# The last four chunks of tile 3 in seven products, in a linear-attention and SwiGLU kernel

## The chip, the cores and the metric

The kernel runs on one core of one Trainium2 chip. The metric is the device time of one execution in microseconds. Before the change the median of three runs is 218.54 us (217.64 to 218.71).

## The reference

Two stages follow each other. The first is linear attention with decay: 4 batches, 8 heads, 768 positions, head dimension 64. In blocks, each head computes a masked and decayed product of q and k, applies it to v, adds q times a running state, and updates the state with k and v:

```python
intra = np.einsum('bhic,bhjc->bhij', qb, kb) * Dmask[None]
intra = np.einsum('bhij,bhjd->bhid', intra, vb)
inter = np.einsum('bhid,bhde->bhie', qb * lam_pow[None], kv_state)
out[:, :, sl] = intra + inter
kv_state = lam_block[None, :, None, None] * kv_state + np.einsum('bhsd,bhse->bhde', kb_dec, vb)
```

Its output, as 3072 tokens of 512 features, is the input of the second stage, a gated feed-forward block of inner width 1536:

```python
g = x @ w_gate
silu = g * (1.0 / (1.0 + np.exp(-g)))
val = x @ w_val
return (silu * val @ w_out).astype(np.float32)
```

## The kernel before

**Groups and tiles.** The attention is done in twelve groups (0 to 11) of 256 tokens, the feed-forward block in six tiles (0 to 5) of 512 tokens. Tile t needs the attention of groups 2t and 2t+1; its input is `xt`. PE works through one list written out by hand: while tile t is in the feed-forward block, the attention of the groups of tile t+1 is put between its steps.

**Attention of a group g.** `load_group` issues the loads of k, q and v (lines 115 and 122), on SP's queue except k of group 11, which ACT issues (`KACT`, line 325). `cast_scaled` (line 277) makes bf16 copies, k on ACT (line 281) and q, scaled, on VectorE or, for groups listed in `QP` (line 275, empty), on GpSimd (line 283); then SP issues a transposing DMA (line 271) that writes `qkt`. `v_scale` (line 258) scales v, mostly on GpSimd. On PE, `scores` (line 376 for groups from 6 on) multiplies q and k, and the masks (line 381) go to VectorE, put off in the list `later`; `inter` (line 502) multiplies q with the state, `intra` (line 515) the masked scores with v; `upd_mm` (line 408) computes the update of the state. ACT copies the update (line 430), GpSimd adds it to the state (line 463), and casts of the state go to `kvn` (lines 443 and 445), for groups 8, 9 and 10 on ACT, queued in `kvq` and let out by `kv_flush` (line 447). `core_a` is `kv_flush`, `inter` and a small guard copy; `core_b` is the waiting masks, `intra` and `evac` (line 527), which writes `xt`. `attend(g)` (line 863) is `core_a(g)`, then `upd_mm`, `upd_copy` and `scores` of g+1, then `core_b(g)` and `state(g+1)`.

**Feed-forward, plain steps.** The inner width has twelve chunks of 128 (`FC`), six in each half (`FH`). A step of a tile does one chunk, `ffn_fc` (line 580): four matmuls of 512 columns for the gate (line 558), Silu on ACT (line 562), four matmuls for the value (line 574), and on VectorE the multiply that writes `h` (line 577). PSUM has eight banks, taken in turn.

**Feed-forward, seven products.** `ffn_unit(t, j, ...)` (line 686) does four chunks at once, 2j and 2j+1 of each half, as a product of two 2x2 block matrices in seven block products in place of eight. Each product is eight matmuls of 256 columns (line 703), four for the gate and four for the value. It needs sums of blocks of the weights (`w_combo`, line 651, n = 0 to 3, on VectorE), sums of blocks of `xt` (`x_combo`, line 672, n = 0 to 3, VectorE), and copies and adds between products: the A products copied bank to bank (line 737) and the E products to `es` (line 740) on ACT, adds on VectorE (lines 745 and 753), four Silus (line 730) on ACT, three multiplies on VectorE and one on GpSimd (line 733). The weight sum n = 3 overwrites a block of the weights, so the plain chunks that use this block must be done before it. `early` and `mid` are functions called after the E products and ahead of the last product. Tiles 4 and 5 are done in three such units each; tiles 0 to 3 in plain steps.

**Output.** For tiles 1 to 5 `out_units` (line 775) multiplies `h` with the output weights, also in seven products per group (line 793), with sums of blocks of `h` (`h_combo`, line 625, line 640) that wait in the list `trickle` and are let out by `drip`.

**What orders the work around the change.** Steps get a number in the order in which they are made; `at(n, fn, ...)` puts a call after step n. Lines 1114 to 1138 make the twelve steps of tiles 2 and 3; tile 3 takes its chunks in an order that goes through both halves two by two (line 1115). `WS` (line 1099) names the step after which each weight sum is computed (301 is step 1 of tile 3, 112 the thirteenth step from the second half of tile 1 on), `AT` (line 1113) the steps after which `attend` is called: for tile 3, `attend(8)` after step 5 and `attend(9)` after step 10. After the loop `out_units(2)` follows (line 1184), with sums for tile 4 let out between its products, and then the units of tile 4 (from line 1201).

Of the kernel before, what the change touches and what calls it, by code (L numbers as in the profile page):

```python
# [9 lines left out]
BF16 = mybir.dt.bfloat16  # L10
# [27 lines left out]
def _body(ctx, tc, nc, q, k, v, lam, moe_w_gate, moe_w_val, moe_w_out, out):  # L38
    B, H, S, D = q.shape
    HP = H // 2  # L40
    BLK = 128
# [4 lines left out]
    FC = DFF // 128  # L46
    FH = FC // 2
# [30 lines left out]
    ring = [0]  # L78

    primed = {}  # L80
# [26 lines left out]
    st = {}  # L107
# [164 lines left out]
                          in_=t.rearrange("p a s x -> p (a s x)"), transpose=True)  # L272
        st[("qkt", g)] = tt

    QP = ()

    def cast_scaled(g, eng=nc.vector):
        eng = nc.gpsimd if g in QP else eng
# [388 lines left out]

    xs = {}
    SY = 1
    XS0 = 4  # L670

    def x_combo(t, n, g):


        xt = st[("xt", t)]
        g = slice(0, 2) if g is None else slice(g, g + 1)
        b11, b12 = xt[:, g, 0:KH, 0], xt[:, g, 0:KH, 1]
        b21, b22 = xt[:, g, KH:MC, 0], xt[:, g, KH:MC, 1]
        if t not in xs:
            pool, tag = (qkt_pool, "qkt") if t == XS0 else (raw_pool, "raw")  # L680
            xs[t] = pool.tile([128, 3, 2, KH, BLK], BF16, name="xs", tag=tag)
        x = [xs[t][:, m, g] for m in range(3)]
        o, i0, i1 = ((x[0], b12, b11), (x[1], b22, x[0]), (x[2], b21, x[1]), (b12, b22, b12))[n]
        nc.vector.tensor_tensor(out=o, in0=i0, in1=i1, op=ALU.subtract)

    def ffn_unit(t, j, bk, early=None, mid=None, dr=(0, 0, 2)):
# [7 lines left out]
        A, E, Bb = [[banks[k] for k in bk[2 * m:2 * m + 2]] for m in range(3)]  # L694
# [5 lines left out]
        def product(i, o, lhs, rhs, start=False):  # L700
            for fi in range(2):
                for c in range(KH):
                    nc.tensor.matmul(o[:, fi * 256:fi * 256 + 256], lhs(i, c, 2 * j + fi), rhs(c),  # L703
                                     start=(start and fi == 0 and c == 0), stop=(c == KH - 1),
                                     skip_group_check=True)
# [10 lines left out]
        def xb(k, r):  # L716
            return lambda c: xt[:, :, KH * k + c, r]
# [18 lines left out]
            product(i, A[i], wa(0, 0), xb(0, 0), True)  # L736
            nc.scalar.copy(out=Bb[i], in_=A[i])
        for i in range(2):
            product(i, E[i], wa(0, 1), xb(0, 1), True)
            nc.scalar.copy(out=es[i], in_=E[i])  # L740
        if early:
            early()
# [264 lines left out]
    def at(n, fn, *a):  # L1007
        plan.setdefault(n, []).append((fn, a))
# [86 lines left out]
    at(s2, h_combo, 1, 0, 1)  # L1095
    at(s2, wo_combo, 3)

    outs = []
    WS = [(x, n, i, 0, 3) for x, n, i in ((110, 0, 0), (112, 0, 1), (206, 1, 0), (210, 1, 1), (301, 2, 0), (303, 2, 1))] + [(308, 3, 0, 0, 2), (309, 3, 1, 0, 2)]
    XC = 8  # L1100
    D0 = (0, 0, 3)
    D1 = (0, 0, 3)
    D5 = 0
    D2 = (0, 0, 2)
    M2 = (1, 1, 0, 2, 1, 2, 2)
# [1 line left out]
    KAGE = 3  # L1107
    KM = 2
    A8 = 5
    A9 = 10  # L1110
    C11 = None
    sns = {0: s1a, 1: s1b + s2h}
    AT = {2: (7, 10), 3: (A8, A9)}
    for t in range(2, 4):
        order = [c for j in range(FC // 4) for c in (2 * j, 2 * j + 1, FH + 2 * j, FH + 2 * j + 1)]
        sn = [step(t, fc, 2 if t == 2 and fc < NH else 0) for fc in (range(FC) if t == 2 else order)]
        sns[t] = sn
        if t == 2:
            at(sn[4], ahead, 6)
        for j, g in ((4 if t == 2 else 0, 2 * t + 3), (8 if t == 2 else 6, 2 * t + 4)):  # L1120
            at(sn[j], cast_scaled, g)
            at(sn[j], load_group, g + 1)
            if g > 7:
                at(sn[1 + j], v_scale, g, nc.gpsimd, 0, H // 2)
                at(sn[(1 if t == 2 else 2) + j], v_scale, g, nc.gpsimd, H // 2, H)
        for i in range(2):
            at(sn[AT[t][i]], attend, 2 * t + 2 + i)
        if t == 2:
            at(sn[4], out_units, 1, (0,), False, 2)
            at(sn[5], out_rest, 1, (0,), 2, 4)  # L1130
            at(sn[6], out_rest, 1, (0,), 4, 7)
            at(sn[5], v_scale, 7, nc.vector)
            at(sn[8], out_units, 1, (1,), False, 2)
            at(sn[9], out_rest, 1, (1,), 2, 7)
            at(sn[9], h_combo, t, (0, 2))
        else:
            at(sn[7], h_combo, t, (0, 2))
        at(sn[11], h_combo, t, 2)
    sn = sns[3]
    if C11 is not None:  # L1140
        at(sn[C11], cast_scaled, 11)
    XM = (1, 1)
    W3L = ()
    TR2 = "cxwh"
    for x, n, i, j0, j1 in WS:
        at(sns[x // 100][x % 100], w_combo, i, n, (j0, j1))
    if not XM[0]:
        for n in (0, 3, 1, 2):
            at(sn[XC], x_combo, 4, n, 0)

    for n, (t, fc, b0, b1) in enumerate(steps):
        if t >= 1 and t + 1 < NG // 2 and ("xt", t + 1) not in st:
            new_xt(t + 1)
        ffn_fc(t, fc, b0, b1)
        kvq_now.append(0)
        kv_flush(KAGE, KM)
        run_later(pace.get(n, 2 if len(later) > 1 else 1))
        todo = plan.get(n, [])
        busy = [f for f, x in todo if f in (attend, ahead, cast_scaled, v_scale)]
        if not busy:  # L1160
            drip(2 if len(trickle) > 4 else 1)
# [12 lines left out]

    def x_soon(t, g):
# [3 lines left out]
              c=[soon(cast_scaled, 11)] if C11 is None else [],  # L1179
# [38 lines left out]
    t = NG // 2 - 1  # L1218
# [38 lines left out]
```

## Time and profile before

| What | Value |
| --- | --- |
| Median of three runs | 218.54 us (217.64 to 218.71) |
| Profiled execution, time | 218.1 us |
| Its span | 216.3 us |
| Granted TensorE clock, mean | 1.0 |
| HBM read and written | 28.31 MB and 6.29 MB |
| Tile 3's twelve steps on PE, with `attend(8)` and `attend(9)` | 111.9 to 135.6 us |
| `out_units(2)` on PE | 135.6 to 144.7 us |
| Tile 4's first two units on PE | 144.7 to 160.2 us |

How to read the profile: times are in microseconds from the start of the span. PE is TensorE's matmuls, PEld its weight loads, DVE VectorE, ACT ScalarE, POOL GpSimd, SP the engine that issues most DMAs; a name with q after it is the engine's sequencer, which issues its DMAs. In the slices each digit is the busy share of one fortieth of the span, in tenths. A row of a timeline has the start, the duration, the engine, the line of the kernel, the operation, what it writes and reads with the shape, the number of merged instructions, and in brackets how long the engine sat idle before it and what ended that. Matmuls overlap in these rows, so start to start is what a stream of them takes.

### The profile page before, as it was taken

How to read it: one execution, taken by the hardware profiler on the slowest of the kernel's cores; microseconds unless marked ns; L12 is line 12 of the kernel's file. 1: busy time of each engine (PE TensorE's matmuls, PEld its weight loads, DVE VectorE, ACT ScalarE, POOL GpSimd, SP SyncE). 2: the span in 40 equal slices, each digit the busy share in tenths (PEclk: the TensorE clock that was granted, in tenths of full speed). 3: DMA queues.
4: the chain of work that ended last, by engine and by line, in shares of the span. 5: the costliest groups of instructions: out<-in, count | busy, mean ns of one | idle time of the engine just before them, and what ended most of it. 6: DMA issues, size and time to landing. Idle time of an engine off the chain costs nothing.

```text
span 216.3 us, 6883 instructions
## 1 busy us (share of the span) xinstructions
PE 209.8 (97%) x2813; PEld 153.3 (71%) x2816; DVE 149.5 (69%) x267; ACT 129.1 (60%) x280; POOL 92.3 (43%) x126
## 2 busy tenths in 40 slices
PE   8899999999999999999999999999999999999994
PEld 4666455888887447666754545888888888888883
DVE  1774447576677989775478988886797379961760
ACT  5788577666545254638368478754872766636522
POOL 6684755818498240685962336510740022200200
PEclk9999999999999999999999999999999999999999
DMA  6999999999999878999678899481000500005014
GB/s 189 346 354 345 378 337 321 290 249 232 315 352 151 191 214 190 257 186 238 168 169 236 203 230 215 103 225 68 2 5 3 194 0 3 0 3 194 0 52 146
DMA packets 88320, 39.76 MB, mean 184 GB/s; under 512 B 57698, under 2 KB 83938, under 8 KB 88290
## 3 DMA queue, kind: packets, MB, share of 16 engines
q1 hardware_dynamic: 84978, 38.22, 64.9%
q10 hardware_dynamic: 3312, 1.11, 2.0%
q8 instruction: 22, 0.36, 0.7%
q14 instruction: 8, 0.07, 0.1%
HBM read 28.31 MB, written 6.29 MB: 160 GB/s over the span
## 4 chain that ended last, share of the span: by engine, by line
PE 73%; DVE 7%; DMA 6%; SPq 5%; ACT 3%; issue 2%; POOL 2%; POOLq 1%; DVEq 0%
PE bank L793 20%; PE bank L703 15%; PE bank L558 13%; PE bank L574 13%; DMA woraw<-in_moe_w_out_dram 4%; PE bank L593 4%; SPq L122 2%; DMA qraw<-in_q_dram 2%; SPq L247 2%; DVE ws L666 2%; DVE h L577 1%; PE bank L515 1%; PE bank L146 1%; DVE wt L623 1%; PE bank L502 1%
## 5 line engine op out<-in xcount | busy, mean ns | idle before, releaser
L577 DVE TENSOR_TENSOR h<-sil,bank 128x256 bf16<-128x256 bf16 (+1 forms) x67 | 34.8, 531 | 26.3 <-PE bank L574 18.0
L558 PE MATMUL bank<-xt,wg_sb 128*128 128x256 bf16 (+1 forms) x268 | 52.5, 319 | 0.0
L574 PE MATMUL bank<-xt,wv_sb 128*128 128x256 bf16 (+1 forms) x268 | 52.4, 319 | 0.0
L562 ACT ACTIVATE sil<-bank 128x256 bf16<-128x256 f32 (+1 forms) x67 | 31.7, 479 | 23.7 <-PE bank L558 16.8
L574 PEld LDWEIGHTS <-wv_sb 128*128 128x128 bf16 x268 | 26.0, 98 | 15.8 <-DVE wv_sb L988 0.5
L558 PEld LDWEIGHTS <-wg_sb 128*128 128x128 bf16 x268 | 25.2, 98 | 13.8 <-DVE xt L527 0.2
L258 POOL TENSOR_TENSOR v_s<-v,dec 128x512 bf16<-128x512 f32 (+1 forms) x18 | 24.1, 1356 | 24.0 <-DMA v<-in_v_dram 16.0
L733 POOL TENSOR_TENSOR h<-sil,es 128x512 bf16<-128x512 bf16 x6 | 7.0, 1163 | 50.0 <-ACT sil L730 50.0
L793 PEld LDWEIGHTS <-h 128*128 128x128 bf16 x240 | 23.3, 98 | 3.4 <-issue 0.3
L793 PE MATMUL bank<-wo_sb,h 128*128 128x256 bf16 x180 | 21.6, 273 | 0.1
L793 PEld LDWEIGHTS <-hs 128*128 128x128 bf16 x180 | 17.6, 98 | 2.9
L357 DVE TENSOR_TENSOR ssb<-bank,causal 128x512 bf16<-128x512 f32 x24 | 15.4, 681 | 1.8 <-PE bank L350 1.8
L745 DVE TENSOR_TENSOR bank<-bank,es 128x512 f32<-128x512 f32 x12 | 7.8, 693 | 11.4 <-PE bank L703 10.1
L703 PEld LDWEIGHTS <-ws 128*128 128x128 bf16 x144 | 13.8, 97 | 2.3 <-issue 0.2
L793 PE MATMUL bank<-wt,hs 128*128 128x256 bf16 x120 | 15.0, 272 | 0.0
L730 ACT ACTIVATE sil<-bank 128x512 bf16<-128x512 f32 x18 | 10.7, 596 | 7.0 <-POOL h L733 4.6
L463 POOL TENSOR_TENSOR kvf<-kvs,ups 128x256 f32<-128x256 f32 x8 | 6.5, 813 | 19.1 <-ACT ups L430 19.1
L733 DVE TENSOR_TENSOR h<-sil,bank 128x512 bf16<-128x512 bf16 x18 | 12.2, 682 | 1.4 <-ACT sil L730 1.4
L703 PE MATMUL bank<-xs,ws 128*128 128x256 bf16 x96 | 12.8, 272 | 0.0
L527 ACT CAST xt<-bank 128x512 bf16<-128x512 f32 x19 | 11.6, 658 | 2.0 <-PE bank L515 1.5
L463 POOL TENSOR_TENSOR kvf<-kvf,ups 128x256 f32<-128x256 f32 x16 | 12.2, 763 | 0.9
L703 PE MATMUL bank<-xt,wg_sb 128*128 128x256 bf16 x72 | 10.8, 273 | 0.2 <-ACT ups L430 0.2
(119 smaller groups left out, 361.3 us busy)
## 6 DMA issues: line engine op xcount, KB each, us to landing
out_dram<-osb SPq DMA_DIRECT2D x22, 256.0 KB, 2.1
v<-in_v_dram SPq DMA_DIRECT2D x18, 256.0 KB, 4.5
woraw<-in_moe_w_out_dram SPq DMA_DIRECT2D x6, 512.0 KB, 7.6
qraw<-in_q_dram SPq DMA_DIRECT2D x24, 128.0 KB, 3.2
wraw<-in_moe_w_gate_dram SPq DMA_DIRECT2D x5, 512.0 KB, 7.2
wraw<-in_moe_w_val_dram SPq DMA_DIRECT2D x5, 512.0 KB, 6.9
kraw<-in_k_dram SPq DMA_DIRECT2D x20, 128.0 KB, 3.1
kraw<-in_k_dram SPq DMA_DIRECT2D x4, 512.0 KB, 6.6
```

The source lines that it names most:

```text
L258: eng.tensor_tensor(out=st[("vs", g)][:, h0:h1], in0=st[("v", g)][:, h0:h1].rearrange("p h (s d) -> p h s d", s=2), in1=vfac(g, h0, h1), o ...
L357: nc.vector.tensor_tensor(out=ssb[:, h2, 2 * c:2 * c + 2].rearrange("p a s n -> p a (s n)"), in0=sp[(c, h2)].rearrange("p (a x) -> p a x", ...
L463: nc.gpsimd.tensor_tensor(out=o, in0=f, in1=u, op=ALU.add)
L527: fns[r](out=xt[:, g % 2, :, r].rearrange("p h (m s) -> p h s m", s=2) if g < NAT0 else xt[:, g % 2, :, :, r * M:r * M + M], in_=op[r].rea ...
L558: nc.tensor.matmul(gp[:, 0:N], wg_sb[:, mc, fs], xt[:, b0 // 2:b1 // 2, mc].rearrange("p g b n -> p g (b n)"), start=(mc == 0), stop=(mc = ...
L562: nc.scalar.activation(sil[:, 0:N], gp[:, 0:N], AF.Silu)
L574: nc.tensor.matmul(vp[:, 0:N], wv_sb[:, mc, fs], xt[:, b0 // 2:b1 // 2, mc].rearrange("p g b n -> p g (b n)"), start=(mc == 0), stop=(mc = ...
L577: nc.vector.tensor_tensor(out=h_sb[:, fc % FH, b0:b1].rearrange("p b n -> p (b n)"), in0=sil[:, 0:N], in1=vp[:, 0:N], op=ALU.mult)
L703: nc.tensor.matmul(o[:, fi * 256:fi * 256 + 256], lhs(i, c, 2 * j + fi), rhs(c), start=(start and fi == 0 and c == 0), stop=(c == KH - 1), ...
L730: nc.scalar.activation(sil[key], src, AF.Silu)
L733: eng.tensor_tensor(out=h_of(half, r), in0=v3(sil[half, r]), in1=v3(src), op=ALU.mult)
L793: nc.tensor.matmul(o, lhs(f), rhs(f), start=(start and f == 0), stop=(f == FH - 1), skip_group_check=True)
```

## The change

Tile 3 keeps its first eight plain steps (chunks 0, 1, 6, 7, 2, 3, 8, 9). Its last four (4, 5, 10, 11) become one `ffn_unit(3, 2, ...)`, in a new function `unit3` called after the loop. `attend(9)` is taken apart: `core_a(9)` is `mid` of the unit, and `upd_mm`, `upd_copy` and `scores` of group 10, then `core_b(9)` and `state(10)`, follow the unit. `early` of the unit lets out the casts of the state of group 9. The six banks of the unit are handed to `out_units(2)`.

The unit needs all weight sums for its columns earlier: n = 1 of the value weights after step 7 of tile 2 instead of step 10, n = 2 after steps 10 and 11 of tile 2 instead of 1 and 3 of tile 3; n = 3 for these columns (2, 3) after steps 0 and 5 of tile 3. The other columns of n = 3 come after tile 3's plain steps, through `W3L` in the list let out during `out_units(2)`. In tile 1 one sum moves from 112 to 111. Weight and x sums are put behind the other calls of their step.

`x_combo` gets a fourth buffer, so that n = 3 no longer overwrites `xt`; for tile 3 the four sums are made after steps 3, 4, 6 and 7. The q of group 10 is cast by GpSimd (`QP = (10,)`). `drip` counts of tile 4's first unit change (`D0`, `E0`).

```diff
-    QP = ()
+    QP = (10,)
...
         if t not in xs:
-            pool, tag = (qkt_pool, "qkt") if t == XS0 else (raw_pool, "raw")
-            xs[t] = pool.tile([128, 3, 2, KH, BLK], BF16, name="xs", tag=tag)
-        x = [xs[t][:, m, g] for m in range(3)]
-        o, i0, i1 = ((x[0], b12, b11), (x[1], b22, x[0]), (x[2], b21, x[1]), (b12, b22, b12))[n]
+            pool, tag = (raw_pool, "raw") if t == 5 else (qkt_pool, "qkt")
+            xs[t] = pool.tile([128, 4, 2, KH, BLK], BF16, name="xs", tag=tag)
+        x = [xs[t][:, m, g] for m in range(4)]
+        o, i0, i1 = ((x[0], b12, b11), (x[1], b22, x[0]), (x[2], b21, x[1]), (x[3], b22, b12))[n]
...
         for i in range(2):
-            product(i, E[i], wa(0, 1), xb(0, 1), True)
+            product(i, E[i], wa(0, 1), xsum(3), True)
...
-    WS = [(x, n, i, 0, 3) for x, n, i in ((110, 0, 0), (112, 0, 1), (206, 1, 0), (210, 1, 1), (301, 2, 0), (303, 2, 1))] + [(308, 3, 0, 0, 2), (309, 3, 1, 0, 2)]
-    XC = 8
-    D0 = (0, 0, 3)
+    def unit3():
+        bk = [(ring[0] + i) % 8 for i in range(6)]
+        ring[0] += 6
+        assert primed[bk[4]] == primed[bk[5]] == 512
+        ffn_unit(3, 2, bk, lambda: (drip(EU[0]), kv_flush()), lambda: (drip(EU[1]), core_a(9)), DU)
+        upd_mm(10)
+        upd_copy(10)
+        scores(10)
+        late, later[:] = later[:], []
+        core_b(9)
+        later[:] = late
+        state(10)
+        st["bk2"] = [bk[n] for n in (4, 0, 2, 5, 1, 3)]
+
+    WS = [(x, n, i, 0, 3) for x, n, i in ((110, 0, 0), (111, 0, 1), (206, 1, 0), (207, 1, 1), (210, 2, 0), (211, 2, 1))] + [(300, 3, 0, 2, 3), (305, 3, 1, 2, 3)]
+    DU = (0, 0, 2)
+    XT = (3, 4, 6, 7)
+    EU = (0, 0)
+    E0 = 4
+    D0 = (0,0,0)
...
-    AT = {2: (7, 10), 3: (A8, A9)}
+    AT = {2: (7, 10), 3: (A8,)}
     for t in range(2, 4):
-        order = [c for j in range(FC // 4) for c in (2 * j, 2 * j + 1, FH + 2 * j, FH + 2 * j + 1)]
+        order = [c for j in range(FC // 4 - 1) for c in (2 * j, 2 * j + 1, FH + 2 * j, FH + 2 * j + 1)]
...
             at(sn[9], h_combo, t, (0, 2))
+            at(sn[11], h_combo, t, 2)
         else:
             at(sn[7], h_combo, t, (0, 2))
-        at(sn[11], h_combo, t, 2)
+            for n, x in enumerate(XT):
+                at(sn[x], x_combo, 3, (0, 3, 1, 2)[n], None)
...
-    W3L = ()
+    W3L = (0, 1)
...
         todo = plan.get(n, [])
+        front = [x for x in todo if x[0] is w_combo or x[0] is x_combo]
+        todo = [x for x in todo if x not in front] + front
...
     run_later(len(later))
+    unit3()
+    run_later(len(later))
     new_xt(5)
...
-    out_units(2, many=list(M2))
+    out_units(2, bk=st["bk2"], many=list(M2))
...
-    trickle[:0] = [soon(w_combo, i, 3, (2, 3)) for i in range(2)]
     def early():
         fixed[:] = [s0, s1]
         scores(11)
+        drip(E0)
```

More of the change, by code (lines that the diff above doesn't have):

```diff
@@ L669, in _body @@
     SY = 1
-    XS0 = 4
     def x_combo(t, n, g):
@@ L1096, in _body @@
     at(s2, wo_combo, 3)
-    outs = []
-    WS = [(x, n, i, 0, 3) for x, n, i in ((110, 0, 0), (112, 0, 1), (206, 1, 0), (210, 1, 1), (301, 2, 0), (303, 2, 1))] + [(308, 3, 0, 0, 2), (309, 3, 1, 0, 2)]
-    XC = 8
-    D0 = (0, 0, 3)
+    def unit3():
[17 more added lines that the diff above has]
+    D0 = (0,0,0)
     D1 = (0, 0, 3)
@@ L1109, in _body @@
     A8 = 5
-    A9 = 10
     C11 = None
     sns = {0: s1a, 1: s1b + s2h}
-    AT = {2: (7, 10), 3: (A8, A9)}
+    AT = {2: (7, 10), 3: (A8,)}
     for t in range(2, 4):
-        order = [c for j in range(FC // 4) for c in (2 * j, 2 * j + 1, FH + 2 * j, FH + 2 * j + 1)]
+        order = [c for j in range(FC // 4 - 1) for c in (2 * j, 2 * j + 1, FH + 2 * j, FH + 2 * j + 1)]
         sn = [step(t, fc, 2 if t == 2 and fc < NH else 0) for fc in (range(FC) if t == 2 else order)]
@@ L1124, in _body @@
                 at(sn[1 + j], v_scale, g, nc.gpsimd, 0, H // 2)
-                at(sn[(1 if t == 2 else 2) + j], v_scale, g, nc.gpsimd, H // 2, H)
-        for i in range(2):
-            at(sn[AT[t][i]], attend, 2 * t + 2 + i)
+                at(sn[1 + j], v_scale, g, nc.gpsimd, H // 2, H)
+        for i, x in enumerate(AT[t]):
+            at(sn[x], attend, 2 * t + 2 + i)
         if t == 2:
@@ L1135, in _body @@
             at(sn[9], h_combo, t, (0, 2))
+            at(sn[11], h_combo, t, 2)
         else:
             at(sn[7], h_combo, t, (0, 2))
-        at(sn[11], h_combo, t, 2)
+            for n, x in enumerate(XT):
+                at(sn[x], x_combo, 3, (0, 3, 1, 2)[n], None)
     sn = sns[3]
-    if C11 is not None:
-        at(sn[C11], cast_scaled, 11)
     XM = (1, 1)
-    W3L = ()
+    W3L = (0, 1)
     TR2 = "cxwh"
@@ L1146, in _body @@
         at(sns[x // 100][x % 100], w_combo, i, n, (j0, j1))
-    if not XM[0]:
-        for n in (0, 3, 1, 2):
-            at(sn[XC], x_combo, 4, n, 0)
     for n, (t, fc, b0, b1) in enumerate(steps):
```

## The prediction

> **What bounds the kernel now.** I read the page's busy shares and slices first, then the timeline of each engine around the change (125 to 161 us), with the built order of both kernels beside it, which names the instruction that each wait stands for.
>
> ```profile
> PE 209.8 (97%) x2813; PEld 153.3 (71%) x2816; DVE 149.5 (69%) x267; ACT 129.1 (60%) x280; POOL 92.3 (43%) x126
> PE   8899999999999999999999999999999999999994
> DVE  1774447576677989775478988886797379961760
> PEclk9999999999999999999999999999999999999999
> ```
>
> PE is full from the third slice to the last but one, at full granted clock: the kernel is as long as PE's list of matmuls plus what PE waits for. What counts is how long PE takes from the eighth step of tile 3 to the start of `out_units(2)`. The timeline of PE, start and duration first:
>
> ```profile
> 127.29 1.03 PE L558 MATMUL bank<-xt,wg_sb 128*128 128x512 bf16 x4
> 128.15 1.03 PE L574 MATMUL bank<-xt,wv_sb 128*128 128x512 bf16 x4
> ...
> 132.84 0.36 PE L408 MATMUL bank<-v_s,qk 64*64 64x64 bf16 x20
> ...
> 133.43 0.49 PE L515 MATMUL bank<-ssb,v_s 64*64 64x64 bf16 x32
> 133.84 1.04 PE L558 MATMUL bank<-xt,wg_sb 128*128 128x512 bf16 x4
> ...
> 135.58 2.78 PE L793 MATMUL bank<-wo_sb,h 128*128 128x256 bf16 x24
> ...
> 147.85 0.60 PE L703 MATMUL bank<-xt,wg_sb 128*128 128x256 bf16 x4
> 148.29 0.60 PE L703 MATMUL bank<-xt,wv_sb 128*128 128x256 bf16 x4
> 148.73 1.04 PE L703 MATMUL bank<-xs,ws 128*128 128x256 bf16 x8
> ```
>
> Durations overlap, so I use start to start: four matmuls of 512 columns take 0.86 (127.29 to 128.15), a seven-product step (eight of 256) 0.88 (147.85 to 148.73). The other engine that matters is ACT:
>
> ```profile
> 125.87 2.12 ACTq L122 DMA_DIRECT2D kraw<-in_k_dram  x3
> 128.09 1.08 ACT L562 ACTIVATE sil<-bank 128x512 bf16<-128x512 f32 x2 [1.40 <-PE bank L574]
> 129.20 0.83 ACT L443 CAST kvn<-kvf 64x256 bf16<-64x256 f32 x2
> 130.06 0.41 ACT L445 CAST kvn<-kvf 128x256 bf16<-128x256 f32 x1
> ...
> 130.98 0.83 ACT L443 CAST kvn<-kvf 64x256 bf16<-64x256 f32 x2
> ...
> 145.44 1.06 ACT L737 COPY bank<-bank 128x512 f32<-128x512 f32 x2
> 146.40 1.09 ACT L740 COPY es<-bank 128x512 f32<-128x512 f32 x2
> ```
>
> ACT issues the loads of k for group 11 until 127.99, so the Silu of the eighth step starts at 128.09 although its matmuls ended near 126.6. Both kernels are alike up to there.
>
> **The change, part by part.**
>
> 1. *Matmuls.* Four steps of eight matmuls go: 2 x 3.45 (two steps, 127.29 to 130.74) = 6.90. Seven steps of 0.873 come: 6.11. **PE saves 0.79 us.** The 24 more weight loads (98 ns each) lie under matmuls spaced 109 ns.
>
> 2. *Attention of group 9 moves into the unit.* The same matmuls, but `inter` now stands before the last product. In `ffn_unit(4, 0)` the product after it took 1.00 (150.94 to 151.94) instead of 0.87: **+0.13**.
>
> 3. *Evacuations inside the unit.* After the Silu at 128.09 (0.48 each, from the pair), ACT does the A copies L737 (0.96 a pair, 145.44 to 146.40), then the E copies L740 (0.95 a pair). PE wants the first copy at 129.04 (127.29 + 2 x 0.875); it ends at 128.09 + 0.48 + 0.60 = 129.17, the second 0.48 later, and the add L745 follows the E copies as closely. PE waits 0.13 + 0.04 + some 0.03: **+0.20**.
>
> 4. *The kv casts.* `early` flushes five casts of group 9's state (L443, L445) on ACT, behind the copies and ahead of all four Silus. Queued behind them are the Silus, behind these the multiplies on DVE, and behind those PE: `upd_mm(10)` and `scores(10)` write the banks that the Silu of the E product and its multiply free. ACT's chain: 128.09 + 0.48 + 0.96 + 0.95 = 130.48; casts 0.86 + 0.31 + 0.82 = 1.99 (rows above), 132.47; Silu (0,0) and (1,1) at 0.54 spacing (two Silus at 150.80 and 151.34), 133.55; Silu (1,0) 0.60, 134.15; multiply L733 on DVE 0.68, **134.83**. Without that wait PE is at `scores(10)` at 127.29 + 6.11 + 0.13 + 0.20 + 0.37 (`inter`, 132.47 to 132.84) + 0.22 (`upd_mm`) = 134.32. **+0.51.** In the kernel before, three of these casts sat between Silus of plain steps, where a ring of eight banks covered them.
>
> 5. *q of group 10 on GpSimd.* Its data lands at 127.45 (DVE's cast starts 127.49 after waiting for it). The one such cast on POOL in the trace, of the same size, and the transposes of these groups:
>
> ```profile
> L283 POOL TENSOR_TENSOR qk<-qraw,dec x1: 1911/1911/1911, 38.5 to 38.5; 128x1024 bf16<-128x1024 f32 x1
> ...
> DMA to landing us min/median/max: 3.7/3.8/4.1
> ```
>
> So 129.40 for the cast instead of 128.64, and the transpose lands by about 133.3 (0.1 for the wait), 1.0 before PE asks at 134.32: nothing now. From the other side: two v_s halves, as many elements, took 2.77 at worst, and with 4.1 for the landing it is 134.5, still under the 134.83 of part 4. Queued behind this cast on POOL are v_s of group 10 (its data came at 130.1 anyway) and the unit's multiply; behind the transpose on SP are q and v of group 11, 0.75 later, q by about 137.3, when DVE reaches its cast. DVE gets 1.14 back, but PE did not wait for DVE there.
>
> The skill says, in "GPSIMD Engine Reference", section 4.1, that a two-input elementwise operation on GpSimd is about twice as slow as on VectorE, which speaks against this move. The trace has 1911 against 1226 ns, 1.56 times. By the rule, as an estimate, the cast would be 2.45 and the landing 133.9; the sum would be the same.
>
> 6. *Weight sums.* Both n=1 and n=2 sums move into tile 2 and early tile 3 (0.87 to 1.8 each on DVE), where DVE sits idle 1.66, 1.63 and 2.70 us ahead of three multiplies (97.8, 101.2, 109.2): nothing, and at worst 0.2 if one of them holds a multiply. The sum moved ahead of a multiply in tile 1 delays that one from 70.0 to 71.4; its bank is wanted at 71.86: nothing. Four halves of n=3 (0.34 each) are now late, in `out_units(2)`; in my walk of DVE the two that `ffn_unit(4, 0)` needs are done near 143.8 and wanted at 145.7. If POOL's v_s holds DVE as it did at 139.13 (an x sum of 0.41 took 1.27), that is 0.9 each time, and twice is still covered.
>
> The skill's "SBUF — State Buffer", section "Who interferes with whom", says that a VectorE instruction with two SBUF inputs and a GpSimd instruction reading SBUF block each other whole. The row at 139.13 agrees in kind. By the rule the third x sum (near 129.3) would wait for POOL's cast to end at 129.4, which leaves the sum as it is.
>
> 7. *x sums of tile 3*, four of 0.33: in DVE's room during tile 3 (it loses more than 3 us of other work there): nothing. If each were held by 0.9, the last would come at 130.6 and cost PE 0.4.
>
> **Sum:** -0.79 + 0.13 + 0.20 + 0.51 = **+0.05 us**. `out_units(2)` then starts at 135.63 instead of 135.58, and every later step is the same work in the same order. What is late next: its second product wants the bank that the last multiply frees at 136.18, and comes at 136.29, so 0.1 of cover. On the profiled execution's 218.1 (span 216.3 and 1.8 around it) this gives 218.15; the median of three, 218.54, lies 0.4 above. I predict **218.5**.
>
> **Rivals.**
>
> - *A, the saving comes through.* If ACT gets to the Silus half a microsecond sooner (casts interleaved with the copies' waits, or the k loads issued sooner), PE does not wait at `scores(10)`: -0.79 + 0.13 + 0.20 = -0.46; with the copies in time too, -0.66, without the switch -0.79. 217.8 to 218.1, say 217.9. For it: my chain has twelve terms and 0.5 to lose. Against it: ACT is in order and each term is a row.
> - *B, slower: the transpose of group 10 is late.* Cast on POOL, transpose, then `scores(10)`; it decides once it lands after 134.83, that is when the cast takes longer than about 3.1 (at a landing of 4.1). A POOL cast of 0.39 elsewhere took 1.27, so 0.88 of holding on top of 2.77 gives a landing of 135.4: +0.6, 219.2. Two such holds, or the same delay handed through SP to group 11's cast and the adds of `out_units(2)` behind it on DVE, give +1.5, 220.0.
> - *C, it doesn't do what it says*: the seven-product steps run slower than 0.873 because weight loads stop hiding. The three undisturbed units ran 168 matmuls in 18.80 (chain, at 169.45), 6.27 each: the saving is 0.63 and the time 218.7.
>
> **How the numbers follow.** Forecast, within 0.4 of no change, and C with it: 0.56. A: 0.25. B: 0.19, of which two thirds beyond 0.5%. A measurement of this kernel tells about 0.5% (1.1 us) from no change; the saving of 0.79 alone can't reach that, so faster needs A and luck of the three runs, whose spread was 1.07: 0.10. Slower by over 0.5%: 0.15 (B's large end and what I have not seen). Same: 0.75. The range takes in A's whole saving below, less some of the runs' spread, and B's small end above: 217.5 to 219.5.
>
> **What would show it.** Right: L703 replacing L558 and L574 from 127.29, `scores(10)` (L376) starting near 134.8 with idle PE before it released by DVE L733, `out_units(2)` at 135.6. The Silus L730 of the unit stand behind five L443 and L445 on ACT. Part 5 is wrong if that wait is released by the transpose; part 6 if L703 waits for L666 near 145.7; part 3 if PE has no gap at 129.0. The prediction is wrong if `out_units(2)` starts before 135.1 or after 136.6, or if a stage after it changes its length by over 0.5.

## The result and the profile after

The changed kernel takes 219.72 us (median of 21 runs, 218.33 to 222.05), the kernel before 218.45 us beside it (21 runs, 217.62 to 219.46). The ratio is 1.0047, with a 95% interval of 1.0029 to 1.0066: slower by about 1 us (0.6 to 1.4), outside the predicted range. Two runs of the changed kernel (222.04 and 222.05) fell into a slower state and are left out of the ratio.

| In the profiled execution | Before | After |
| --- | --- | --- |
| Time | 218.10 us | 220.19 us |
| Span | 216.3 us | 217.9 us |
| Time less span | 1.8 us | 2.3 us |
| Start of the stretch (ninth step, or the unit) | 127.29 us | 127.68 us |
| Stretch: from there to `out_units(2)` | 8.29 us | 9.41 us (forecast 8.34) |
| `out_units(2)` to `out_units(3)` | 24.53 us | 24.60 us |

The 0.39 us ahead of the unit can't be laid on the change: the changed trace is 1.68 us behind already at the plain step that starts at 57.16 us before and 58.84 after, ahead of the first sum that the change moves (near 70 us), and over all profiles the start of `out_units(0)` lies between 87.0 and 89.3 us. What the change does to PE is in the stretch. The traced pair exaggerates it: the traced execution before lies 0.35 us under its median, the changed one 0.47 over its own. Of the 1 us in the ratio, 0.42 lies outside the span (mean of all runs, further below), which leaves about 0.6 for the span, where the traced pair shows 1.6.

One edit stands neither in the list nor in the shortened diff above: the second half of `v_scale` in tile 3 goes to GpSimd one step earlier, with the first half. Four line numbers move: the products are now L702, the copies L736 and L739, the multiplies L732, `out_units` L792.

The page's busy shares and clock show a PE as full as before, at full clock:

```profile
PE 209.4 (96%) x2837; PEld 155.4 (71%) x2840; DVE 151.9 (70%) x275; ACT 131.0 (60%) x284; POOL 96.6 (44%) x128
...
PEclk9999999999999999999999999999999999999999
```

The timeline of PE in the stretch:

```profile
127.68 0.60 PE L702 MATMUL bank<-xt,wg_sb 128*128 128x256 bf16 x4
...
128.99 0.60 PE L702 MATMUL bank<-xs,wv_sb 128*128 128x256 bf16 x4
130.45 1.08 PE L702 MATMUL bank<-xs,ws 128*128 128x256 bf16 x8 [0.87 <-ACT bank L736]
...
134.56 1.05 PE L702 MATMUL bank<-xt,ws 128*128 128x256 bf16 x8
...
136.42 0.44 PE L376 MATMUL bank<-qkt 64*64 64x64 bf16 x30 [0.42 <-DVE h L732]
...
137.09 2.86 PE L792 MATMUL bank<-wo_sb,h 128*128 128x256 bf16 x24
```

Two waits stand in it, both forecast in kind: ahead of the third pair of products, for ACT's first copy, and at `scores(10)`, for a multiply. The first was forecast at 0.2 us and is 1.0 (128.99 + 0.44 = 129.43, start at 130.45). Why ACT is late is in the chain of work that ended last (start, duration, what; "issue" is time in which the engine waited for nothing that the profile shows):

```profile
123.99 4.54 DMA qraw<-in_q_dram
128.53 0.04 issue
128.57 0.65 ACTq L122
...
129.32 0.04 ACT sil L562
...
129.81 1.08 ACT bank L736 x2
...
135.68 0.70 DVE h L732
...
136.42 0.44 PE bank L376 x30
```

The chain into `out_units(2)` begins at a DMA: the last load of q of group 10, issued on SP. It lands at 128.53. Only then does ACT issue its last load of k of group 11 (`ACTq L122`), and only behind that does the Silu of the eighth step start, at 129.32, whose matmuls had ended some two microseconds earlier. In the built order this wait is written: the fourth of ACT's loads waits for the landing of SP's last q load of group 10, because SP's and ACT's DMAs take their semaphores in turn from one small set. Both kernels have that wait. In the kernel before the load had landed by 127.49, when DVE's cast of it starts, 0.20 us after the ninth step began; here it lands 0.85 us after the unit began, and ACT is released 0.7 us after the landing (0.65 for the issue).

### The profile page after: what moved, and what is told of

Same layout as the page of the kernel before. It is cut to its first block, busy times and chain, and to the rows that moved or that the text cites. A ratio compares the mean times of both kernels' runs of the same rounds, so it can differ in the third digit from the quotient of the medians.

```text
span 217.9 us, 6949 instructions
## 1 busy us (share of the span) xinstructions
PE 209.4 (96%) x2837; PEld 155.4 (71%) x2840; DVE 151.9 (70%) x275; ACT 131.0 (60%) x284; POOL 96.6 (44%) x128
## 4 chain that ended last, share of the span: by engine, by line
PE 74%; DMA 10%; SPq 7%; ACT 4%; issue 2%; DVE 1%; POOL 1%; POOLq 1%; ACTq 0%; DVEq 0%
PE bank L792 21%; PE bank L702 15%; PE bank L558 14%; PE bank L574 13%; DMA qraw<-in_q_dram 6%; PE bank L593 5%; DMA wraw<-in_moe_w_val_dram 3%; SPq L115 3%; SPq L233 3%; PE bank L515 2%; ACT sil L729 1%; PE bank L502 1%; PE bank L350 1%; PE bank L408 1%; SPq L122 1%
## 5 line engine op out<-in xcount | busy, mean ns | idle before, releaser
L577 DVE TENSOR_TENSOR h<-sil,bank 128x256 bf16<-128x256 bf16 (+1 forms) x63 | 32.2, 524 | 26.8 <-PE bank L574 17.8
L558 PE MATMUL bank<-xt,wg_sb 128*128 128x256 bf16 (+1 forms) x252 | 48.4, 315 | 0.0
L574 PE MATMUL bank<-xt,wv_sb 128*128 128x256 bf16 (+1 forms) x252 | 48.3, 315 | 0.0
L562 ACT ACTIVATE sil<-bank 128x256 bf16<-128x256 f32 (+1 forms) x63 | 29.4, 472 | 24.8 <-PE bank L558 17.1
L558 PEld LDWEIGHTS <-wg_sb 128*128 128x128 bf16 x252 | 23.7, 98 | 12.0 <-DVE xt L527 0.2
L732 POOL TENSOR_TENSOR h<-sil,es 128x512 bf16<-128x512 bf16 x7 | 8.2, 1165 | 51.1 <-ACT sil L729 49.7
L792 PEld LDWEIGHTS <-h 128*128 128x128 bf16 x240 | 23.2, 98 | 3.3 <-issue 0.3
L792 PE MATMUL bank<-wo_sb,h 128*128 128x256 bf16 x180 | 21.7, 272 | 0.1
L792 PEld LDWEIGHTS <-hs 128*128 128x128 bf16 x180 | 17.6, 98 | 2.9
L702 PEld LDWEIGHTS <-ws 128*128 128x128 bf16 x168 | 16.0, 97 | 3.7 <-issue 1.2
L729 ACT ACTIVATE sil<-bank 128x512 bf16<-128x512 f32 x21 | 12.5, 594 | 7.7 <-POOL h L732 5.4
L732 DVE TENSOR_TENSOR h<-sil,bank 128x512 bf16<-128x512 bf16 x21 | 14.3, 684 | 2.9 <-ACT sil L729 2.4
L702 PE MATMUL bank<-xs,ws 128*128 128x256 bf16 x112 | 15.0, 272 | 0.9 <-ACT bank L736 0.9
L463 POOL TENSOR_TENSOR kvf<-kvf,ups 128x256 f32<-128x256 f32 x16 | 15.2, 948 | 0.9
L792 PE MATMUL bank<-wt,hs 128*128 128x256 bf16 x120 | 15.0, 272 | 0.0
L702 PEld LDWEIGHTS <-wg_sb 128*128 128x128 bf16 x112 | 10.9, 98 | 1.9 <-issue 0.3
```

Of the source, the lines that this page charges most:

```text
L463: nc.gpsimd.tensor_tensor(out=o, in0=f, in1=u, op=ALU.add)
L558: nc.tensor.matmul(gp[:, 0:N], wg_sb[:, mc, fs], xt[:, b0 // 2:b1 // 2, mc].rearrange("p g b n -> p g (b n)"), start=(mc == 0), stop=(mc = ...
L562: nc.scalar.activation(sil[:, 0:N], gp[:, 0:N], AF.Silu)
L574: nc.tensor.matmul(vp[:, 0:N], wv_sb[:, mc, fs], xt[:, b0 // 2:b1 // 2, mc].rearrange("p g b n -> p g (b n)"), start=(mc == 0), stop=(mc = ...
L577: nc.vector.tensor_tensor(out=h_sb[:, fc % FH, b0:b1].rearrange("p b n -> p (b n)"), in0=sil[:, 0:N], in1=vp[:, 0:N], op=ALU.mult)
L729: nc.scalar.activation(sil[key], src, AF.Silu)
```

## Theory, rivals and the experiments

**Theory T**: ACT's queue stands at the k loads until q of group 10 has landed; in the unit everything behind them (Silu, copies, kv casts, four Silus) comes late by as much, and PE with it. **Rival B**: GpSimd's cast of q and the transpose behind it set the end. **Rival V**: the sums that moved on DVE do. A fourth question is what the kv casts cost.

All runs, "stretch" as above, "Silu" the start of the eighth step's Silu less the start of the stretch, "outside" the mean of time less span over the runs of that kernel:

| Run | What | Ratio to before (95%) | Stretch, us | Silu, us | Outside, us |
| --- | --- | --- | --- | --- | --- |
| before | | 1 | 8.29 | +0.80 | 1.74 |
| changed | | 1.0047 (1.0029 to 1.0066) | 9.41 | +1.64 | 2.16 |
| e15 | changed, again | 1.0069 (1.0046 to 1.0092) | 9.30 | +1.52 | 2.16 |
| e1 | k of 11 on SP | 1.0017 (0.9992 to 1.0042) | 7.94 | -0.64 | 1.89 |
| e2 | e1, casts early | 1.0011 (0.9981 to 1.0040) | 8.36 | +0.39 | 1.90 |
| e7 | e1, three casts early | 1.0027 (0.9994 to 1.0060) | 7.92 | +0.42 | 1.92 |
| e6 | two k loads on ACT | 1.0036 (1.0002 to 1.0070) | 7.96 | -0.65 | 2.00 |
| e5 | casts early, k on ACT | 1.0109 (1.0068 to 1.0150) | 9.72 | +1.74 | 2.10 |
| e4 | q cast on DVE | 1.0053 (1.0024 to 1.0083) | 8.82 | +1.06 | 2.37 |
| e9 | k on GpSimd, q cast on DVE | 1.0042 (1.0010 to 1.0073) | 9.11 | -0.67 | 2.06 |
| e12 | e1, q cast on DVE | 1.0033 (1.0012 to 1.0054) | 9.22 | -0.66 | 2.07 |
| e3 | before, k of 11 on SP | 1.0095 (1.0057 to 1.0133) | 9.56 | -0.59 | 1.75 |
| e10 | before, two k loads | 1.0001 (0.9967 to 1.0034) | 9.07 | -0.60 | 1.75 |
| e8 | before, early weight sums | 1.0017 (0.9978 to 1.0055) | 8.39 | +0.71 | 1.75 |
| e13 | before, q cast on GpSimd | 1.0040 (1.0014 to 1.0066) | 9.72 | +1.99 | 1.73 |
| e14 | before, four x buffers | 1.0011 (0.9983 to 1.0040) | 8.69 | +1.46 | 1.74 |
| e11 | before, idle matmuls | 0.9973 (0.9950 to 0.9996) | 8.28 | +1.02 | 1.74 |

The last row calibrates the others. It changes nothing ahead of the last product, and still reads 0.27% faster, so two ratios within 0.3% of each other tell nothing here; the stretch, read inside one trace, tells more, but of one execution. Taken together the ratios do fall in order: the four versions with the unit that free ACT and leave the cast of q on GpSimd (e1, e2, e6, e7) read 1.0011 to 1.0036, the four in which ACT is held (changed, e15, e4, e5) 1.0047 to 1.0109, though single intervals overlap.

### ACT's queue (e1, e5, e6, e15)

**e1**, the changed kernel:

```diff
-    KACT = (11,)
+    KACT = ()
...
+            if g == 10:
+                at(sn[j], load_group, 11, "k")
             at(sn[j], cast_scaled, g)
-            at(sn[j], load_group, g + 1)
+            at(sn[j], load_group, g + 1, "qv" if g == 10 else "kqv")
```

> The changed kernel, with the four loads of k for group 11 issued on SP (ahead of the transpose of group 10, where SP is idle from 127.70 to 130.71 in the changed kernel's trace) instead of on ACT between steps 7 and 8. Theory T (ACT is held at these loads until 129.3, 1.64 us after the unit's first matmul, and everything behind them on ACT comes late): the Silu of the eighth step starts within 0.3 us of the unit's first matmul, PE's extra 0.9 us ahead of the third pair of products shrinks to 0.2 or less, and the time from the unit's first matmul to the first out_units(2) matmul falls from 9.41 to between 7.6 and 8.1 us; time 1.3 to 1.8 us under the changed kernel's, 0.3 to 0.8 us under the kernel before's. Rival B (the cast on GpSimd and the transpose of group 10 set the end): scores(10) waits as before, for the transpose; 9.0 to 9.5 us, no gain on the changed kernel, or a loss, as the transpose now has four more loads ahead of it on SP. Rival V (the sums that DVE took on): no change from the changed kernel.

The timelines of PE and of ACT in e1:

```profile
128.04 0.60 PE L702 MATMUL bank<-xt,wg_sb 128*128 128x256 bf16 x4
...
129.35 0.60 PE L702 MATMUL bank<-xs,wv_sb 128*128 128x256 bf16 x4
129.78 1.04 PE L702 MATMUL bank<-xs,ws 128*128 128x256 bf16 x8
130.66 0.60 PE L702 MATMUL bank<-xt,wg_sb 128*128 128x256 bf16 x4
...
135.98 2.86 PE L792 MATMUL bank<-wo_sb,h 128*128 128x256 bf16 x24
```

```profile
127.40 0.59 ACT L562 ACTIVATE sil<-bank 128x512 bf16<-128x512 f32 x1
128.73 1.06 ACT L736 COPY bank<-bank 128x512 f32<-128x512 f32 x2 [0.74 <-PE bank L702]
```

The Silu starts ahead of the unit, ACT now waits for PE, and PE's gap is gone (129.35 + 0.43 = 129.78). The stretch is 7.94 us, 1.47 under the changed kernel's and 0.35 under the kernel before's. The time fell by about 0.7 us by the two ratios, half of the 1.3 to 1.8 expected and at the edge of what they can tell, and stayed level with the kernel before.

**e6** frees ACT without touching SP: two loads of 128 partitions each, of which the second waits for the first q load instead of the last. It leaves out the reversed order of the second block's heads.

```diff
-            for p0, n, rev in parts:
+            for p0, n, rev in [(0, 128, False)] if what == "kraw" and g == 11 else parts:
```

> The changed kernel with k of group 11 loaded on ACT by two DMAs of 128 partitions instead of four of 64 (the same bytes; the second block's heads are not put in reversed order, so that part of the attention is not the reference's). SP's order is untouched. As built, the second load waits for the landing of the first q load of group 10 instead of the last. Theory T: ACT is free 1 to 2 us earlier than in the changed kernel, the Silu of the eighth step starts -0.5 to +0.4 us from the unit's first matmul, the gap ahead of the third pair is 0.3 or less, the unit's start to out_units(2) is 7.8 to 8.4 us (9.41), time 1.0 to 1.6 us under the changed kernel's. Rival B: unchanged within 0.3 us.

Silu at -0.65, no gap, 7.96 us: in the stretch the same as e1 by another way. The time missed: 1.0036 is 0.2 us under the changed kernel's, where 1.0 to 1.6 were expected. **e5** was to move the hold in the other direction; as built, the last k load then waits for a load of v.

```diff
-        kv_flush(KAGE, KM)
+        kv_flush(1 if t == 3 and fc in (8, 9) else KAGE, KM)
```

> The changed kernel with the kv casts of group 9 given to ACT one or two steps earlier and the k loads of group 11 left on ACT. As built, ACT's fourth k load then waits for the landing of the first v load of group 10 instead of the last q load of group 10. It is a dose of the held time. Theory T (ACT's queue, and every instruction behind the loads, stands until that landing, plus 0.5 us): the v load lands about 5.7 us after its issue, some 3 us after the unit's first matmul, so the Silu of the eighth step starts 3 to 3.5 us after it (1.64 in the changed kernel), PE's gap ahead of the third pair of products grows from 0.9 to 2 to 3 us, and the unit's start to out_units(2) becomes 10 to 11 us (9.41), 0.6 to 1.6 us slower than the changed kernel, although the casts are out of the unit. If only the issue time of the loads counts, or the casts in the unit: 7.6 to 8.6 us, 0.8 to 1.8 us faster than the changed kernel.

The timelines of PE and of ACT in e5:

```profile
129.13 0.60 PE L702 MATMUL bank<-xt,wg_sb 128*128 128x256 bf16 x4
...
132.84 1.07 PE L702 MATMUL bank<-xs,ws 128*128 128x256 bf16 x8 [1.80 <-ACT bank L736]
```

```profile
129.10 1.67 ACTq L122 DMA_DIRECT2D kraw<-in_k_dram  x2
130.87 0.60 ACT L562 ACTIVATE sil<-bank 128x512 bf16<-128x512 f32 x1 [1.12 <-PE bank L702]
```

The row of the Silu names PE for ACT's idle time, but the last thing to end ahead of it is ACT's own last load, at 130.77. PE's gap doubles (130.44 + 0.44 = 130.88, start at 132.84: 1.96 us) and the stretch is 9.72 us although three casts left the unit. The v load landed sooner than I had said, so Silu and stretch miss their windows, and the run is not the dose that it was meant to be: the Silu is only 0.1 us later than in the changed kernel, and 0.8 us of the longer gap are the two casts that now stand between it and the copies. What e5 does show is that taking casts out of the unit, with ACT still held, shortens nothing; the 7.6 to 8.6 us of the other reading is out. The time is 0.6% over the changed kernel's, of which the stretch is a third of a microsecond; the rest is not explained. **e15** is the changed kernel again.

> The changed kernel again. Theory T: in this second profile too the last k load on ACT ends 0.4 to 0.5 us after q of group 10 has landed, and the Silu of the eighth step starts 0.1 us after that, whatever the landing; the unit's start to out_units(2) is 7.8 us plus as much as that Silu starts later than the unit's first matmul, so 8.6 to 9.6 us. Outside the span 1.9 to 2.35 us.

GpSimd's cast, which waits for the same landing, starts at 128.99; ACT's last load ends at 129.37, 0.38 later; the Silu starts at 129.47, 1.52 after the unit, and the stretch is 9.30 (7.8 + 1.52 = 9.32). T's rule, taken from the changed kernel and e4, holds within 0.1 us in a second execution. In e4 DVE waits for the same landing, until 129.36, ACT's loads end at 129.86, and 7.8 + 1.06 = 8.86 stands beside 8.82.

### GpSimd's cast and the transpose (e4, e9, e12, e13)

**e4** is the changed kernel with `QP = ()`, so that DVE casts q of group 10.

> The changed kernel with q of group 10 cast on DVE again, as in the kernel before; everything else as changed. Theory T: nothing on the way to out_units(2) waits for this cast, so the time is the changed kernel's within 0.3 us (DVE takes 1.2 us more, 0.2 us at worst of it ahead of the unit's multiplies). Rival B: the transpose lands 0.7 us sooner and the time falls by 0.6 us or more; out_units(2) then starts near 8.6 us after the unit's first matmul instead of 9.4.

The time is the changed kernel's. The row of PE behind the gap:

```profile
131.10 1.08 PE L702 MATMUL bank<-xs,ws 128*128 128x256 bf16 x8 [0.28 <-ACT bank L736]
```

The stretch is 0.59 shorter, near the number that I had written for B, but by T: PE's wait at `scores(10)` is 0.42 us and for the multiply in both, and the whole difference lies in the gap ahead of the third pair (0.45 against 1.02), because q landed about half a microsecond sooner against the unit. B is out for the changed kernel. **e9** puts the k loads on GpSimd's queue, **e12** on SP's as in e1, both with the cast on DVE:

```diff
-                load_fp32(g, nc.scalar if what == "kraw" and g in KACT else nc.sync, src, what)
+                load_fp32(g, nc.gpsimd if what == "kraw" and g in KACT else nc.sync, src, what)
```

> The changed kernel with k of group 11 loaded by GpSimd's queue, so that neither ACT nor SP stands at it, and q of group 10 cast on DVE (so that GpSimd has nothing between step 6 and v_s of group 10 but these loads). As built, the loads on GpSimd wait for no load of group 10. Theory T: the Silu of the eighth step starts before the unit's first matmul, no gap ahead of the third pair, unit's start to out_units(2) 7.8 to 8.1 us (9.41 in the changed kernel, 7.94 to 7.96 in the two experiments that freed ACT); SP's order is that of the changed kernel, so the stretch from out_units(2) to out_units(3) stays at 24.5 to 24.6 us. Time 1.2 to 1.7 us under the changed kernel's. If GpSimd's loads land too late for the cast of k of group 11 on ACT, or slow GpSimd's v_s: 24.8 us or more in that stretch, or scores(10) waits.

> The first experiment (k of group 11 on SP) with q of group 10 cast on DVE again. In the ninth experiment DVE stood at this cast until its data had landed, the third and fourth x sum came after it, and PE waited 0.52 us for them and 0.48 for the adds. If that is general once ACT is not held: unit's start to out_units(2) 8.7 to 9.2 us, PE waiting for DVE, 0.8 to 1.2 us slower than the first experiment (7.94). If GpSimd's cast was worth nothing, as my fifth and seventh steps had it: 7.8 to 8.1 us.

In e9 the Silu is early (-0.67), and yet the stretch is 9.11 us, and the time, expected 1.2 to 1.7 us lower, is the changed kernel's. The timelines of PE and of DVE in e9:

```profile
129.68 1.05 PE L702 MATMUL bank<-xs,ws 128*128 128x256 bf16 x8 [0.52 <-DVE xs L683]
...
132.08 1.19 PE L702 MATMUL bank<-xs,ws 128*128 128x256 bf16 x8 [0.48 <-DVE bank L744]
```

```profile
128.06 1.22 DVE L283 TENSOR_TENSOR qk<-qraw,qdn 128x1024 bf16<-128x1024 f32 x1 [0.98 <-DMA qraw<-in_q_dram]
```

DVE now is the engine in order that stands at a load: it waits 0.98 us for q, casts, and only then makes the x sums that PE's next product reads. e12 repeats it with e1's loads. Its rows of DVE and of PE:

```profile
129.40 0.42 DVE L683 TENSOR_TENSOR xs<-xt,xs 128x512 bf16<-128x512 bf16 x1
...
129.87 1.05 PE L702 MATMUL bank<-xs,ws 128*128 128x256 bf16 x8 [0.88 <-ACT es L739]
```

The row names ACT's copy to `es`, which ends within 0.02 us of DVE's sum; in e1 the same product starts a microsecond before that copy ends, so it is the sum that PE waits for. The stretch is 9.22 against 7.94: in these traces the cast on DVE costs 1.28 us once ACT is free, and nothing while ACT is held longer (e4). The two ratios, 0.16% apart, can't show it. **e13** is the kernel before with `QP = (10,)`.

> The kernel before with q of group 10 cast on GpSimd. For the time outside the span: 1.74 us if the cast has no part in it, 1.9 or more if it has. In the span: the transpose 0.7 us later, which PE waits for if it lands after 132.9 us (scores(10) there), so 0 to 1 us slower.

There the cast on GpSimd is a loss: PE waits 0.46 us for the transpose and 0.24 for v_s, and a Silu held until +1.99 makes `inter` wait 0.21 for a kv cast; the stretch is 9.72. So rival B's mechanism is real where `scores(10)` stands early; with the unit it stands 1.2 us (e1) to 3.0 us (changed) later against the start of the stretch.

### Was the hold a cost before? (e3, e10)

**e3** is e1's edit in the kernel before, **e10** e6's.

> The kernel before with the same move of the four k loads of group 11 from ACT to SP. Theory T: the plain steps there have eight banks of cover, PE had no wait behind the Silu of step 8, so the time stays within 0.3 us of the kernel before's. If it gains 0.5 us or more, the held ACT queue was a cost in both kernels and the first experiment's gain says nothing on the change.

> The kernel before with k of group 11 loaded by two DMAs on ACT instead of four (same bytes; the second block's heads are not reversed, so that part of the attention is not the reference's). SP's order is untouched, other than in the third experiment, which delayed a transpose. As built, neither of the two loads waits for a load of group 10, so ACT is free about 1.5 us sooner. Theory T: the plain steps were covered by the eight banks, PE gains nothing: within 0.3 us of the kernel before. If the hold was a cost in both kernels: 0.5 us or more faster.

e3 missed: 0.95% slower, some 2.1 us, of which the stretch shows 1.27. The timelines of SP and of PE in e3 say where those come from:

```profile
127.54 3.01 SPq L122 DMA_DIRECT2D kraw<-in_k_dram  x4
130.72 2.16 SPq L271 DMA_TRANSPOSE qkt<-qk  x1
```

```profile
134.97 0.45 PE L376 MATMUL bank<-qkt 64*64 64x64 bf16 x32 [0.87 <-DMA qkt<-qk]
```

SP is busy with the k loads for 3.01 us, and the transpose behind them starts at 130.72 instead of 128.86. e1 has the same loads, but there GpSimd's cast ends at 130.30 anyway. e10 leaves SP alone and the time is the same (1.0001), as expected. Its reason is not as clean: PE came 0.88 us earlier to the ninth step than in the kernel before and then waited for v_s of group 10, whose data had landed at 130.58, so the stretch grew to 9.07. In the kernel before these loads are just on time.

The cleaner answer is in e14 and e11, made for another question (below): there ACT's loads are the kernel before's. The timeline of ACT in e14:

```profile
125.51 2.77 ACTq L122 DMA_DIRECT2D kraw<-in_k_dram  x3
128.38 1.09 ACT L562 ACTIVATE sil<-bank 128x512 bf16<-128x512 f32 x2 [2.13 <-PE bank L558]
```

The ninth step begins at 126.92, so the Silu is 1.46 us late, nearly as late as in the changed kernel (1.52 and 1.64), and 1.02 in e11. PE waits for nothing of ACT's in either stretch; 8.69 us in e14 comes with a wait for v_s at `upd_mm`, and e11 has 8.28. So the plain steps cover a hold of this size, and the unit does not. At 1.99 (e13) it shows there too, with the 0.21 us at `inter`.

### The casts, the sums and the rest (e2, e7, e8, e14, e11)

**e2** is e1 with e5's line, **e7** the same line with `fc == 8` alone.

> As the first experiment, and besides the five kv casts of group 9 are given to ACT one or two steps earlier, ahead of the unit's copies, instead of between the copies and the four Silus. It asks what the casts inside the unit cost once ACT is not held. If my fourth step was right (+0.51 us from the casts alone): with the casts still inside (first experiment) PE waits about 0.5 us less the 0.5 to 0.9 that ACT gains, so nothing, and this one is equal to the first within 0.2 us. If ACT's chain from the copies to the third Silu is still what scores(10) waits for in the first experiment, this one is 0.3 to 0.6 us faster than it. If the early casts hold the copies, it is 0.2 to 0.5 slower.

> As the first experiment (k of group 11 on SP), with three of the five kv casts given to ACT after step 6 instead of inside the unit, so that, other than in the second experiment, no cast stands right ahead of the unit's copies. Expected: no gap ahead of the third pair (0.44 us in the second experiment) and no wait at scores(10): unit's start to out_units(2) 7.55 to 7.75 us (7.94 in the first, 8.36 in the second, 8.29 in the kernel before), so 0.5 to 0.7 us under the kernel before if nothing else in the change costs. If the time stays at or above the kernel before's, some other stage of the change loses the difference.

In e2 two casts stand right ahead of the copies and PE waits 0.44 us for them: 8.36. In e7 no cast does, and the wait at `scores(10)` is gone, but the stretch is e1's (7.92): what the chain gains, PE loses inside the unit, where a product after the adds starts 0.15 us late. So moving the casts out of the unit gains nothing once ACT is free. e7 missed its window by 0.2, and its time, expected 0.5 to 0.7 us under the kernel before's, is not under it; there `out_units(2)` to `out_units(3)` takes 24.91 us. **e8** is the kernel before with the weight sums of n = 1 and 2 moved as in the change.

> The kernel before with only the change's earlier weight sums of n = 1 and n = 2 (in tile 2 and tile 1 instead of up to step 3 of tile 3, put behind the other calls of their step); no unit in tile 3. My sixth step said nothing: within 0.3 us of the kernel before. If DVE is delayed in tile 2 and hands that to PE: 0.4 to 0.8 us slower, and PE idles released by DVE between 90 and 126 us.

Its ratio holds 1, and PE has no wait above 0.2 us between 90 and 126 us: rival V is out for these sums, by the trace rather than by the ratio, whose interval reaches 0.55%. **e14** gives the kernel before the fourth x buffer (the diff of the change), **e11** 24 matmuls and weight loads behind the last product.

> The kernel before with the fourth buffer for the x sums (tiles 4 and 5), so that the last sum no longer overwrites xt. For the time outside the span: 1.74 us if the buffers have no part in it, 1.9 or more if they have. In the span: within 0.3 us.

> The kernel before with 24 tiny matmuls (64x64 by 8 columns) and their 24 weight loads added on PE after the last product, where PE has nothing left to do and the last output is still being stored; PE then has as many instructions as in the changed kernel. It asks where the time outside the span comes from: all runs of the kernel before and of two variants of it show 1.74 us (1.67 to 1.85) between the span and the time, the changed kernel 2.16 (1.85 to 2.35), and no row of a trace covers it. If it goes with the number of PE's instructions: 1.9 us or more here. If not: 1.74, and the span the same within 0.2 us.

These two and e13 look for the time outside the span. In 118 runs of the kernel before it is 1.67 to 1.85 us, in its six variants no different; in the changed kernel it is 1.85 to 2.35 and in every variant of that 1.89 to 2.37 in the mean. None of the early sums, the cast, the buffers and the number of PE's instructions brings it by itself. It is there in every program with the unit in tile 3 and in no other, is 0.42 us of the changed kernel's loss, and no trace covers it. Its cause stays open.

## Why the prediction was wrong

The step that failed is part 3, with the sentence under the rows of ACT: "ACT issues the loads of k for group 11 until 127.99, so the Silu of the eighth step starts at 128.09 ... Both kernels are alike up to there." The code up to there is alike, the time is not. I took the end of ACT's loads as a place on PE's clock. It is the landing of a load on another queue, which the chain shows and the built order states as a wait. In the kernel before that landing lay 0.20 us behind the start of the ninth step; in its variants e8, e3 and e14 it is 0.06, 0.74 and 0.86, so one profile gave the favourable end (each by the start of the cast that reads q; e11, the same code up to the last product, has 0.42). What made it a cost is the unit: the plain steps cover a Silu 1.46 us late (e14), while in the unit the stretch grows with it one for one (8.82 us at +1.06, 9.30 at +1.52, 9.41 at +1.64).

By the steps:

- *Matmuls*: right. A seven-product step in e1 takes 0.88 us (129.78 to 130.66), 0.873 forecast; rival C is out.
- *`inter` in the unit*: right. The product after it takes 0.97 us (134.56 to 135.53), 1.00 forecast.
- *Evacuations*: mechanism right, size wrong: 1.02 us for 0.20, by the 0.84 us (1.64 less 0.80) that the Silu came later. In e4, with the Silu at +1.06, the gap is 0.45, as the forecast's own sum gives with 0.26 more. From e1 and e6: with the Silu early the gap is nothing.
- *kv casts*: the wait at `scores(10)` and its chain are as forecast, in the order forecast. From that Silu to `scores(10)` the chain took 7.10 us, 6.74 forecast, 0.36 more, spread over starts of instructions. `scores(10)` to `out_units(2)` took 0.67 instead of 0.80.
- *Sum*: +0.05 + 0.84 + 0.36 - 0.13 = +1.12 us, the stretch's 9.41 less 8.29 in the two traced executions.
- *q on GpSimd*: right that PE does not wait for the transpose. DVE's cast ends at 128.72 by its row, not 128.64, which changes nothing. "PE did not wait for DVE there" held only under the held ACT (e4); without it the cast on GpSimd is worth 1.28 us (e1 against e12).
- *Weight sums, x sums*: right, nothing, while ACT is held (e8; no wait for L666 in the changed kernel).
- *Around the span*: the second step that failed. I carried 1.8 us over unchanged, without a reason; it is 2.16 in the mean, and why stays open.

Rival A's condition, "the k loads issued sooner", was the right one. Met in e1, it gave -0.35 us in the stretch for the -0.46 forecast. But the time outside the span takes 0.15 of that back, and the ratio can't show the remaining 0.2: none of these versions is faster than the kernel before.

The Trainium skill's "Trainium Kernel Development and Optimization", section "Key Constraints", says that issuing DMAs from several engines only saves the sequencer's issue time. Here it saved that on SP (the four loads take 2.92 us there in e1). It also put the same loads, with a wait for another queue's data, in front of ACT's compute, which cost 1.47 us of the stretch between the traces of e1 and of the changed kernel.

## What to carry over

A DMA issued from a compute engine's queue is a wait of that engine: before putting latency-bound work behind it, look in the built order for what it waits, and take its release as an offset from that landing, with its spread over several traces, and not as a time. Queue depth hides such a hold (eight banks in plain steps, 1.46 us in e14), and a unit that hands banks back through the same engine uncovers it. When one holder is taken away, look which in-order engine stands at the same data next: here ACT, then SP or DVE.

## What was not expected of the hardware

- The release of ACT follows the landing of q closely in all eight executions whose last k load on ACT waits for it: 0.29 (e13) to 0.55 us (e8) after the cast that reads q started (before 127.49 and 127.99, e4 129.36 and 129.86, e15 128.99 and 129.37).
- The loads of q reached the cast that waits for them 3.34 us (before) and 4.23 us (e11) after the end of their last issue, with the same code up to the last product; over the other versions it is 3.15 (e3) to 4.50 (e12). The DMA engines are busy for 0.89 and 1.02 of the stretch (changed and before), which fits loads that wait for one another; no run separates that.
- On GpSimd's queue the four loads took 2.89 us (e9, 126.30 to 129.19), and started without waiting for q of group 10, for which DVE's cast waits until 128.06.
- The time outside the span is a property of the program: 1.73 to 1.75 us in the mean in seven programs, 1.89 to 2.37 in nine others that share the unit in tile 3.
